# Ones beside the values written once, values split in pieces of 512 columns, and a plan whose clock begins later

## The chip, the core and the metric

The kernel runs on one core of a Trainium2 chip. The core has five engines with a program each: TensorE (PE, matrix products), VectorE (DVE), ScalarE (ACT), GpSimd (POOL) and SyncE (SP, which issues the DMAs). Each engine works through its program in order; one engine waits for another through semaphores. The metric is device microseconds (us) of one execution. Of the kernel before there are three timed runs, with a median of 378.32 us, and one profiled execution.

## The reference

The computation is a chain of three blocks in fp32, for batch 2, 768 positions and 512 channels:

```
scores = q k^T / 8 - slope_h * dist              # 8 heads of 64, keys: 8 global, 96 local
a = softmax(scores where kept, else -1e9);  x = a v      # (2, 768, 512)
h = relu(x w_in);  c = conv over 3 positions of h, per channel
x = (h * sigmoid(c)) w_out                               # (2, 768, 512)
u, v = split(relu(x w_in2));  v = layernorm(v)
x = (u * (w_spatial v + b)) w_out2
```

Each position attends at most to the 8 first keys and to the 96 last ones, so the scores are computed in bands of 256 keys for every 128 queries.

## The kernel before

**The split in halves.** An fp32 matrix is written as a high half in fp16 and a low half, the rest, in fp16 too. A product of two such matrices is three fp16 products: high by high, high by low, low by high. `parts` makes the two halves: a copy to the high half (`copy`, on ACT or DVE), then source minus high half (`minus`, on POOL or DVE; with a scale on DVE alone). Weights arrive from HBM in fp64 and are decoded first (`decode`: POOL, ACT, DVE, DVE), in 16 blocks of w_in and w_out, each 512 KB.

**The attention.** It goes by 6 groups g (2 batches of 3 chunks of 256 positions). A group has 4 pairs of heads, so there are 24 units u, each of two steps of 128 queries: scores on PE (L838), lowest score and difference on DVE (L857), exponential on ACT (L875), turned probabilities, weighing with the values on PE (`weigh`), norm on DVE (L955 to L960), and a turn into the x of the next block (L991). Groups 0 and 1 (`PLAINS`) take values and probabilities in fp32 (L943; the probabilities are turned by PE, L888). Groups 2 to 5 take halves (L949 to L951; the probabilities are turned by a DMA on SP, L914).

**The values.** There is one buffer `v` for the values of a group, in fp32, and two buffers each for `vh` and `vl`, their halves. Each pair of heads has 130 columns in `v` (groups 0, 1) or `vh`: a one, 128 values, a one. The ones make a product with the probabilities give their sum beside the weighed values. `v_load` loads a group; `ones_beside` writes the ones with a memset on POOL; `v_split` makes the halves of groups 2 to 5 (L507 on ACT for `vh`, L519 on DVE for `vl`), and `watch_values` sums squares of `vh` on PE (L796). A load into `v` has to wait until the group before has been read: by `weigh` for groups 0 and 1, by L519 for the others.

**The order.** Nothing runs at once when it is written. Each step is a task of the `Plan`, with a cost for each engine that could do it. `order` makes a list schedule by these costs, several times with other priorities, some of them drawn at random with a fixed seed, and keeps the one that ends first by its own count. The engines' programs are then written in that order, and the engines keep to it, whatever the true times. So a cost that is altered can move instructions everywhere. Behind the plan stands another layer, which puts in the semaphores that the memory accesses need, in the order in which they are written. Where the plan has room on PE in its first 70 us (`WARM_TO`), `emit` fills it with products of no use (`warm`, L1036), into a PSUM bank of their own.

**After the attention** come the first block's products (`inner`, L1065, and `outer`, L1135, which begin during the attention), and the second block (L1219, L1429, L1341, L1491).

Of the kernel before, what the change touches and what calls it, by code (L numbers as in the profile page):

```python
# [23 lines left out]
B, H, S, D = 2, 8, 768, 64  # L24
DM, DFF = 512, 1024
P = 128
NPAIR = H // 2
# [20 lines left out]
NATS, PLAINS = (0, 1, 2), (0, 1)  # L48
# [5 lines left out]
HALF = dict(w=8, x=9, h=12, y=12, g=12, v=8, s=16)  # L54
# [26 lines left out]
def act_bank(n):  # L81
    return 0.06 + 0.00082 * n
# [10 lines left out]
def dve(n):  # L93
    return 0.07 + 0.00105 * n


def beside(n):

    return 0.1 + 0.0022 * n
# [4 lines left out]


def pool(n):
    return 0.15 + 0.0019 * n


def copy_cost(n):  # L110
    return dict(ACT=act(n), DVE=fast(n))


def sub_cost(n):
    return dict(POOL=pool(n), DVE=beside(n))


class Plan:
# [5 lines left out]
    ENGINES = ("PE", "DVE", "ACT", "POOL", "SP")  # L124
    AFTER = dict(PE=0.21, DVE=0.13, ACT=0.14, POOL=0.1, SP=0.03)
    ISSUE, FLIGHT, LANDING, RATE = 0.45, 0.7, 0.9, 0.41e6

    def __init__(self, tc, room):
        self.tc, self.room = tc, room
        self.tasks, self.touched, self.count, self.over, self.slot = [], {}, {}, {}, {}  # L130

    def next(self, kind):
        n = self.count.get(kind, 0)
        self.count[kind] = n + 1
        return kind, n
# [115 lines left out]
    def trial(self, late, total):  # L251

        tasks, after = self.tasks, self.after
        n = len(tasks)
        waits = [len(t[2]) for t in tasks]
        ready = [0.0] * n
        free = dict.fromkeys(self.ENGINES, 0.0)
        banks = [(0.0, k) for k in range(7)] + [(WARM_TO, 7)]
        uses, slots, ended = dict(self.uses), {}, {}
        self.final = final = [0.0] * n  # L260
        dma = 0.0
        open_ = {i for i in range(n) if not waits[i]}
        result = []

        while open_:
            best = None
            for e in self.ENGINES:
                mine = []
                for i in open_:
                    costs = tasks[i][0]  # L270
                    if e not in costs:
                        continue
                    start = max(free[e], ready[i])
                    k = len(self.opens[i])
                    if k:
                        if len(banks) < k:
                            continue
                        start = max(start, banks[k - 1][0])
                    if e == "SP":
                        start = max(start, dma - self.ISSUE - self.FLIGHT - SLACK)  # L280
                        if total:
                            start = max(start, total + late[i] - AHEAD)
                    margin = -MARGIN if e == "DVE" else MARGIN
                    if any(
                        max(free[f], ready[i]) + c + margin < start + costs[e] for f, c in costs.items() if f != e
                    ):
                        continue
                    mine.append((start, i))
                if mine:
                    soon = min(s for s, _ in mine)  # L290
                    rank = lambda i: (
                        late[i] + BIAS * (e == "DVE" and len(tasks[i][0]) > 1)
                        - CLOSE * (e != "PE" and len(self.users[i]) > 0)
                    )
                    i = min((i for s, i in mine if s <= soon + 1e-9), key=rank)
                    soon = next(s for s, j in mine if i == j)
                    if best is None or soon < best[0]:
                        best = soon, e, i
            start, e, i = best
            costs, _, _, load = tasks[i]  # L300
            end = free[e] = start + costs[e]
            if e == "SP":
                dma = max(dma, end + self.FLIGHT) + load
                end = dma + self.LANDING
            result.append((i, e, start))
            final[i] = end
            for k in self.opens[i]:
                slots[k] = banks.pop(0)[1]
            for k in self.users[i]:
                ended[k] = max(ended.get(k, 0.0), end)  # L310
                uses[k] -= 1
                if not uses[k]:
                    banks.append((ended[k] + self.AFTER[e], slots[k]))
                    banks.sort()
            open_.remove(i)
            for j in after[i]:
                waits[j] -= 1
                ready[j] = max(ready[j], end + (0.0 if e == "PE" and "PE" in tasks[j][0] else self.AFTER[e]))
                if not waits[j]:
                    open_.add(j)  # L320
        return result, max(free.values()), slots

    def emit(self, keep=True, warm=None):

        if not keep:
            for costs, emit, _, _ in self.tasks:
                emit(next(iter(costs)))
            return
        block = self.tc.nc.cur_bb.bb
        last = {}  # L330
        seen = len(block.instructions)
        order = self.order()
        when = {i: (start, start + self.tasks[i][0][e]) for i, e, start in order}
        busy, each = 0.0, 0.213
        for i, e, start in order:
            if e == "PE":
                if start < WARM_TO:
                    for _ in range(int((start - busy) / each)):
                        warm()
                    if each > 0.2 and busy > 0:  # L340
                        for _ in range(WARM_AGAIN):
                            warm()
                        each = 0.107
                busy = max(busy, when[i][1])
            self.tasks[i][1](e)
            traced = block.instructions
            for ins in traced[seen:]:
                if ins.engine in last:
                    self.tc.add_manual_dep(
                        ins, last[ins.engine],  # L350
                        mybir.DependencyInfo(mybir.DependencyClass.NoSync, mybir.DependencyReason.DATA),
                        reason="planned order",
                    )
                last[ins.engine] = ins.name
            seen = len(traced)
# [33 lines left out]
class Kernel:  # L389
# [181 lines left out]
    def parts(self, n, hi, lo, src, reads, wh, wl, scale=1.0):  # L571

        add = self.plan.add
        psum = callable(src)
        get = src if psum else lambda: src
        add(
            dict(ACT=act_bank(n), DVE=dve(n)) if psum else copy_cost(n), lambda e: self.copy(e, hi, get(), scale),
            reads=reads, writes=wh,
        )
        add(  # L580
            dict(DVE=dve(n) if psum or n > 512 else dve(n) + 0.3) if psum or scale != 1.0 else sub_cost(n),
            lambda e: self.minus(e, lo, get(), hi, scale),
            reads=list(reads) + list(wh), writes=wl,
        )
# [166 lines left out]
    def v_load(self, g):  # L751
        b, c = divmod(g, NCH)
        n = 3 if c == 0 else 4
        if g in PLAINS:
            v = self.m("v").rearrange("p (n d) -> p n d", d=VW)
            self.ones_beside(v, ("v", g, "one"))
            self.load(
                v[:, : n * NPAIR, 1 : 1 + 2 * D], self.vb[b, c, :, :n].rearrange("p a (n d) -> p (a n) d", d=2 * D),
                [("v", g, "v")], n * P * 2048,
            )  # L760
            return
        v = self.m("v")[:, :2048].rearrange("p (a n) -> p a n", a=4)[:, :n]
        self.load(v, self.vb[b, c, :, :n], [("v", g)], n * P * 2048)
# [11 lines left out]
    def v_split(self, g):  # L775

        if g in PLAINS:
            return
        n = 3 if g % NCH == 0 else 4
        vh, vl = self.v_halves(g)  # L780
        v = self.m("v")[:, : n * 512].rearrange("p (n d) -> p n d", d=2 * D)
        self.ones_beside(vh, ("vh", g, "one"))
        vh, vl = vh[:, : n * NPAIR, 1 : 1 + 2 * D], vl[:, : n * NPAIR]
        self.parts(n * 512, vh, vl, v, [("v", g)], [("vh", g, "v")], [("vl", g, "v")], 2.0 ** HALF["x"])
        self.watch_values(g, vh, n * NPAIR)

    def watch_values(self, g, vh, n):
# [246 lines left out]
    def warm(self):  # L1034

        self.nc.tensor.matmul(self.bank[:, 7, : 2 * P], self.some[:, :P], self.some, start=True, stop=True)  # L1036
# [730 lines left out]
```

## Time and profile before

| what | value |
|---|---|
| timed runs, median (lowest to highest) | 378.32 us (377.89 to 378.91) |
| the profiled execution: time, and span from first to last instruction | 377.42 us, 375.3 us |
| PE busy, share of the span | 356.9 us, 95% |
| ACT, DVE, POOL busy | 275.1, 266.1, 222.4 us (73%, 71%, 59%) |
| mean granted TensorE clock | 0.989 |
| HBM read and written | 31.48 MB, 3.15 MB |

The span is what the trace shows; 2.1 us of the profiled execution's time lie around it. The profiled execution is 0.90 us (0.24%) shorter than the median of the runs. "Busy" for PE is a modelled time: products overlap, and one that is listed with 273 ns follows the one before it by some 110. An engine's idle time is listed with the instruction that it waited for. [...]

### The profile page before, as it was taken

What the parts mean: (1) busy time and instruction counts of PE and PEld (TensorE: products, weight loads), DVE (VectorE), ACT (ScalarE), POOL (GpSimd) and SP (SyncE); (2) the same over time, 40 slices, a digit from 0 to 9 for tenths busy, and PEclk for the clock granted to TensorE, in tenths of its full rate; (3) what the DMA queues carried; (4) which work ended last, traced back from release to release, by engine and by line L of the source; (5) the groups of instructions that cost most, each with busy time, mean ns of one, the idle gap of its engine ahead of it and who ended that gap; (6) DMA issues with size and microseconds to landing.
All of it is one profiled execution on the core that took longest, in us unless ns stands there. A gap on an engine that the chain in (4) does not pass through costs nothing.

```text
span 375.3 us, 8187 instructions
## 1 busy us (share of the span) xinstructions
PE 356.9 (95%) x2928; PEld 255.8 (68%) x2928; DVE 266.1 (71%) x698; ACT 275.1 (73%) x692; POOL 222.4 (59%) x326
## 2 busy tenths in 40 slices
PE   8999499999979999999999999999999999999993
PEld 5787387777768787888788866676546666664442
DVE  5787599558897797999899576357499998881000
ACT  5898499988986898999899566469985846574221
POOL 5654756575468679998866122139985699652000
PEclk9999699999999999999999999999999999999999
DMA  7989511289929796487557000000054000001222
GB/s 222 402 284 290 194 38 38 75 208 224 213 77 220 148 252 186 86 171 213 113 73 211 2 1 2 0 3 0 10 173 152 19 0 2 0 2 56 114 99 79
DMA packets 46257, 43.63 MB, mean 116 GB/s; under 512 B 34816, under 2 KB 36608, under 8 KB 45696
## 3 DMA queue, kind: packets, MB, share of 16 engines
q1 hardware_dynamic: 46208, 43.03, 42.2%
q8 instruction: 25, 0.41, 0.5%
q14 instruction: 24, 0.20, 0.2%
HBM read 31.48 MB, written 3.15 MB: 92 GB/s over the span
## 4 chain that ended last, share of the span: by engine, by line
PE 78%; ACT 7%; DMA 5%; POOL 4%; issue 2%; DVE 2%; SPq 0%; POOLq 0%; ACTq 0%; DVEq 0%
PE bank L1065 13%; PE bank L1341 11%; PE bank L1135 10%; PE bank L1491 8%; PE bank L1429 8%; PE bank L1219 8%; PE bank L838 6%; PE bank L943 5%; DMA v_dt_float<-in_vb 2%; PE bank L1036 2%; DMA pt_dt_float<-ph_dt_float 2%; PE bank L888 2%; POOL hl_dt_float L523 1%; PE bank L949 1%; PE bank L991 1%
## 5 line engine op out<-in xcount | busy, mean ns | idle before, releaser
L1065 PE MATMUL bank<-x_dt_float,w1h_dt_float 128*128 128x260 f16 (+1 forms) x384 | 66.7, 277 | 5.4 <-DVE wk_dt_float L707 5.4
L1135 PE MATMUL bank<-hl_dt_float,w2h_dt_float 128*128 128x254 f16 (+2 forms) x192 | 52.3, 272 | 3.5 <-POOL hl_dt_float L523 3.1
L1065 PE MATMUL bank<-x_dt_float,w1l_dt_float 128*128 128x260 f16 (+1 forms) x192 | 53.0, 276 | 0.0
L1078 DVE SCALAR_TENSOR_TENSOR bank<-hp_dt_float,cwt,bank 128x254 f32<-128x254 f32 (+2 forms) x96 | 46.6, 487 | 8.4 <-ACT bank L1072 5.7
L1135 PE MATMUL bank<-hh_dt_float,w2h_dt_float 128*128 128x254 f16 (+2 forms) x192 | 52.4, 273 | 0.0
L1135 PE MATMUL bank<-hh_dt_float,w2l_dt_float 128*128 128x254 f16 (+2 forms) x192 | 52.3, 272 | 0.0
L523 POOL TENSOR_TENSOR hl_dt_float<-ac_dt_float,hh_dt_float 128x256 f16<-128x256 f32 (+2 forms) x47 | 34.3, 735 | 27.9 <-ACT hh_dt_float L509 24.2
L1065 PEld LDWEIGHTS <-w1h_dt_float 128*128 128x128 f16 x384 | 37.0, 99 | 12.5 <-issue 6.5
L523 POOL TENSOR_TENSOR ph_dt_float<-sb_dt_float,ph_dt_float 128x512 f16<-128x512 f32 x30 | 34.9, 1167 | 13.8 <-ACT ph_dt_float L509 13.4
L857 DVE CUSTOM_DVE_ANT_0 sb_dt_float<-bank,bias_dt_float 128x256 f32<-128x256 f32 (+1 forms) x96 | 35.0, 402 | 10.2 <-PE bank L838 5.8
L1135 PEld LDWEIGHTS <-w2h_dt_float 128*128 128x128 f16 x384 | 36.1, 98 | 7.4 <-issue 1.7
L875 ACT ACTIVATE sb_dt_float<-sb_dt_float,nb_dt_float 128x256 f32<-128x256 f32 (+1 forms) x64 | 29.2, 491 | 9.3 <-POOL nb_dt_float L870 7.0
L1429 PE MATMUL bank<-ys_dt_float,w3uh_dt_float 128*128 128x384 f16 x128 | 31.2, 326 | 0.0
L1491 PE MATMUL bank<-w4h_dt_float,g_dt_float 128*128 128x512 f16 (+1 forms) x104 | 28.9, 363 | 0.0
L1219 PE MATMUL bank<-w3vh_dt_float,ys_dt_float 128*128 128x512 f16 x96 | 28.6, 379 | 0.0
L696 POOL TENSOR_SCALAR raw_dt_float<-raw_dt_float 128x512 int32<-128x512 uint8 x28 | 20.8, 743 | 10.9 <-DMA raw_dt_float<-in_w 9.2
L1491 PEld LDWEIGHTS <-g_dt_float 128*128 128x128 f16 x156 | 15.2, 98 | 15.8
L1341 PE MATMUL bank<-ws_dt_float,vn_dt_float 128*128 128x384 f16 x144 | 24.9, 326 | 0.0
L1219 PEld LDWEIGHTS <-ys_dt_float 128*128 128x128 f16 x144 | 14.1, 98 | 15.6
L1098 ACT ACTIVATE bank<-bank 128x254 f32<-128x254 f32 (+2 forms) x48 | 17.8, 371 | 8.7 <-DVE bank L1078 8.7
L1072 ACT ACTIVATE bank<-hp_dt_float,cwt 128x254 f32<-128x254 f32 (+2 forms) x48 | 23.3, 485 | 0.4
L507 ACT ACTIVATE wk_dt_float<-bank 128x512 f32<-128x512 f32 (+1 forms) x13 | 7.3, 564 | 22.2 <-PE bank L1491 22.2
(182 smaller groups left out, 998.4 us busy)
## 6 DMA issues: line engine op xcount, KB each, us to landing
raw_dt_float<-in_w SPq DMA_DIRECT2D x20, 512.0 KB, 5.4
qk_dt_float<-in_qk SPq DMA_DIRECT2D x24, 336.0 KB, 3.9
v_dt_float<-in_vb SPq DMA_DIRECT2D x4, 1024.0 KB, 5.7
out_x<-wk_dt_float SPq DMA_DIRECT2D x11, 256.0 KB, 2.0
raw_dt_float<-in_wst SPq DMA_DIRECT2D x6, 384.0 KB, 3.9
raw_dt_float<-in_w3v SPq DMA_DIRECT2D x4, 512.0 KB, 5.1
raw_dt_float<-in_w3u SPq DMA_DIRECT2D x4, 512.0 KB, 5.5
v_dt_float<-in_vb SPq DMA_DIRECT2D x2, 768.0 KB, 5.7
```

The lines of the kernel that those rows point to most:

```text
L523: self.engines[e].tensor_tensor(out=out, in0=in0, in1=in1, op=ALU.subtract)
L838: nc.tensor.matmul(self.ps(sp[h])[:, :256], x[r, t * P : (t + 1) * P], y[r, k0 : k0 + 256], start=n == 0, stop=n == len(pairs) - 1,)
L857: nc.vector.tensor_tensor_reduce(out=sb[:, h, :n], in0=self.ps(self.sp[s][h])[:, :n], in1=self.m("bias", 2 * p + h)[:, t0 : t0 + n], scale ...
L875: nc.scalar.activation(out=sb[:, h, :n], in_=sb[:, h, :n], func=AF.Exp, scale=-1.0, bias=nb[:, h : h + 1])
L1065: nc.tensor.matmul(self.ps(acc)[:, :nx], w[f][:, k * P : (k + 1) * P], x[:, k, x0:], start=k == n == 0, stop=k == 3 and n == 2,)
L1072: nc.scalar.activation(out=ac(), in_=near(1), func=AF.Copy, scale=tap(1))
L1078: nc.vector.scalar_tensor_tensor(out=ac(), in0=near(j), scalar=tap(j), in1=ac(), op0=ALU.mult, op1=ALU.add)
L1135: nc.tensor.matmul(ps(), w[2 * d + k // 4][:, k % 4 * P : (k % 4 + 1) * P], x, start=k == n == 0, stop=k == 7 and n == 2,)
L1219: nc.tensor.matmul(ps(), x[:, y, k, tk], w[k], start=n == 0, stop=n == 11)
L1341: self.nc.tensor.matmul(self.ps(acc)[:, :HS], v[:, k, x, ek], w[:, k, y], start=n == 0, stop=n == 8)
L1429: nc.tensor.matmul(ps(), w[e4][:, k * P : (k + 1) * P], x[:, y, k, s], start=n == 0, stop=n == 11)
L1491: nc.tensor.matmul(ps(), x[:, y, k, tk], w[k][:, at], start=n == 0, stop=n == 11)
```

## The change

There are four edits.

1. `v_load` writes the ones beside the values for group 0 alone; groups 1 and those after leave them where they are, and the load names the memset of its group as something to wait for. `v_split` writes them for groups 2 and 3 alone, which are the first users of the two `vh` buffers.
2. `v_split` makes the halves in pieces of 512 columns (one block of 128 keys) in place of 2048 or 1536 at once: 4, 3, 4 and 4 pieces for groups 2 to 5.
3. Costs in the plan: the clock of every engine begins at 0.75 us and that of the DMA at 3.2 us instead of 0; POOL's cost has a further term above 512 columns; a scaled `minus` from SBUF costs 0.1 us over its line instead of 0.3 us (up to 512 columns) or nothing (above).
4. `emit` fills 0.8 of the room on PE with products of no use instead of all of it.

```diff
 def pool(n):
-    return 0.15 + 0.0019 * n
+    return 0.15 + 0.0019 * n + 0.001 * max(n - 512, 0)
...
+    BEGIN, FIRST = 0.75, 3.2
...
-        free = dict.fromkeys(self.ENGINES, 0.0)
+        free = dict.fromkeys(self.ENGINES, self.BEGIN)
...
-        dma = 0.0
+        dma = self.FIRST
...
-                    for _ in range(int((start - busy) / each)):
+                    for _ in range(int(0.8 * (start - busy) / each)):
                         warm()
...
-            dict(DVE=dve(n) if psum or n > 512 else dve(n) + 0.3) if psum or scale != 1.0 else sub_cost(n),
+            dict(DVE=dve(n) if psum else dve(n) + 0.1) if psum or scale != 1.0 else sub_cost(n),
...
             v = self.m("v").rearrange("p (n d) -> p n d", d=VW)
-            self.ones_beside(v, ("v", g, "one"))
+            if g == 0:
+                self.ones_beside(v, ("v", g, "one"))
             self.load(
                 v[:, : n * NPAIR, 1 : 1 + 2 * D], self.vb[b, c, :, :n].rearrange("p a (n d) -> p (a n) d", d=2 * D),
-                [("v", g, "v")], n * P * 2048,
+                [("v", g, "v")], n * P * 2048, [("v", g, "one")],
             )
...
         vh, vl = self.v_halves(g)
-        v = self.m("v")[:, : n * 512].rearrange("p (n d) -> p n d", d=2 * D)
-        self.ones_beside(vh, ("vh", g, "one"))
-        vh, vl = vh[:, : n * NPAIR, 1 : 1 + 2 * D], vl[:, : n * NPAIR]
-        self.parts(n * 512, vh, vl, v, [("v", g)], [("vh", g, "v")], [("vl", g, "v")], 2.0 ** HALF["x"])
+        v = self.m("v")[:, :2048].rearrange("p (n d) -> p n d", d=2 * D)
+        if g - len(PLAINS) < self.m.at["vh"][2]:
+            self.ones_beside(vh, ("vh", g, "one"))
+        vh = vh[:, :, 1 : 1 + 2 * D]
+        for j in range(n):
+            at = slice(j * NPAIR, (j + 1) * NPAIR)
+            self.parts(
+                512, vh[:, at], vl[:, at], v[:, at], [("v", g), ("vh", g, "one")], [("vh", g, "v", j)], [("vl", g, "v", j)],
+                2.0 ** HALF["x"],
+            )
```

**What moves on POOL, while the weights are decoded.** `raw` holds a block of weights as it came, `w1l` is the low half of a block of w_in. In the program before, the second memset of `v`, that of group 1, stands between two blocks:

```order
L696 TENSOR_SCALAR raw_3_dt_float32_134<-raw_3_dt_float32_134 128x512
L696 TENSOR_SCALAR raw_4_dt_float32_139<-raw_4_dt_float32_139 128x512
L768 MEMSET v_0_dt_float32_86 128x16x2
L696 TENSOR_SCALAR raw_5_dt_float32_140<-raw_5_dt_float32_140 128x512
L523 TENSOR_TENSOR w1l_5_dt_float32_100<-wk_1_dt_float32_126,w1h_5_dt_float32_92 128x512
L523 TENSOR_TENSOR w1l_6_dt_float32_101<-wk_2_dt_float32_133,w1h_6_dt_float32_93 128x512
```

In the changed program the same place, with lines numbered one higher there:

```order
L524 TENSOR_TENSOR w1l_4_dt_float32_99<-wk_0_dt_float32_124,w1h_4_dt_float32_91 128x512
L697 TENSOR_SCALAR raw_4_dt_float32_139<-raw_4_dt_float32_139 128x512
L524 TENSOR_TENSOR w1l_5_dt_float32_100<-wk_1_dt_float32_126,w1h_5_dt_float32_92 128x512
L697 TENSOR_SCALAR raw_5_dt_float32_140<-raw_5_dt_float32_140 128x512
L524 TENSOR_TENSOR w1l_6_dt_float32_101<-wk_2_dt_float32_133,w1h_6_dt_float32_93 128x512
```

The memset is gone, and the decoding is followed by the same subtractions, a little interleaved. On PE the program before holds 106 products of no use, the changed one 85.

**What moves on SP, at the first DMA transposes (group 2).** `pt` and `ph` are turned and unturned probabilities, the v load is that of group 2. Before:

```order
L567 DMA qk_0_dt_float32_85<-in_qk 128x672
L914 DMA_TRANSPOSE pt_0_dt_float32_128<-ph_0_dt_float32_201 128x16x128
L567 DMA v_0_dt_float32_86<-in_vb 128x2048
L914 DMA_TRANSPOSE pt_1_dt_float32_141<-ph_1_dt_float32_203 128x16x128
L567 DMA qk_1_dt_float32_119<-in_qk 128x672
L567 DMA qk_2_dt_float32_127<-in_qk 128x672
L567 DMA v_0_dt_float32_86<-in_vb 128x1536
```

Changed:

```order
L568 DMA qk_0_dt_float32_85<-in_qk 128x672
L568 DMA v_0_dt_float32_86<-in_vb 128x2048
L922 DMA_TRANSPOSE pt_0_dt_float32_128<-ph_0_dt_float32_201 128x16x128
L568 DMA qk_1_dt_float32_119<-in_qk 128x672
L922 DMA_TRANSPOSE pt_1_dt_float32_141<-ph_1_dt_float32_203 128x16x128
L568 DMA qk_2_dt_float32_127<-in_qk 128x672
L568 DMA v_0_dt_float32_86<-in_vb 128x1536
```

The load of group 2's values, which waits for the last weighing of group 1, moved ahead of the first transpose, and a load of q and k moved between the two transposes.

**What moves on DVE, where the low half of group 4's values is made** (`x` is the next block's input, `sb` and `nm` belong to scores). Before:

```order
L1103 SCALAR_TENSOR_TENSOR ac_0_dt_float32_176<-bank_74,hp_0_dt_float32_175 128x256
L523 TENSOR_TENSOR x_1_dt_float32_153<-bank_74,x_0_dt_float32_152 128x256 x2
L519 SCALAR_TENSOR_TENSOR vl_0_dt_float32_147<-v_0_dt_float32_86,vh_0_dt_float32_146 128x2048
L857 ISA sb_0_dt_float32_120,nm_3_dt_float32_142<-bank_74,bias_2_dt_float32_79 128x256
L857 ISA nm_3_dt_float32_142 128x1
```

Changed:

```order
L520 SCALAR_TENSOR_TENSOR vl_0_dt_float32_147<-v_0_dt_float32_86,vh_0_dt_float32_146 128x512
L865 ISA sb_0_dt_float32_120,nm_3_dt_float32_142<-bank_74,bias_2_dt_float32_79 128x256
L865 ISA nm_3_dt_float32_142 128x1
L865 ISA sb_0_dt_float32_120,nm_3_dt_float32_142<-bank_74,bias_3_dt_float32_80 128x256
L865 ISA nm_3_dt_float32_142 128x1
L865 ISA sb_1_dt_float32_129,nm_4_dt_float32_144<-bank_74,bias_4_dt_float32_81 128x160
L865 ISA nm_4_dt_float32_144 128x1
L865 ISA sb_1_dt_float32_129,nm_4_dt_float32_144<-bank_74,bias_5_dt_float32_82 128x160
L865 ISA nm_4_dt_float32_144 128x1
L520 SCALAR_TENSOR_TENSOR vl_0_dt_float32_147<-v_0_dt_float32_86,vh_0_dt_float32_146 128x512 x2
L520 SCALAR_TENSOR_TENSOR ys0_0_dt_float32_202<-bank_74,ys0_0_dt_float32_202 128x254
L520 SCALAR_TENSOR_TENSOR vl_0_dt_float32_147<-v_0_dt_float32_86,vh_0_dt_float32_146 128x512
```

One instruction became four, with work for the scores between them. From the first product of the second block (L1219) on, PE's program is the same in both.

## Rows read from the trace of the kernel before

**Rows 1.** The page, part 1: busy us, share of the span, instructions.

```profile
PE 356.9 (95%) x2928; PEld 255.8 (68%) x2928; DVE 266.1 (71%) x698; ACT 275.1 (73%) x692; POOL 222.4 (59%) x326
```

**Rows 2.** Stretches: us, busy of PE, PEld, DVE, ACT, POOL, granted clock, DMA.

```profile
36.70:42.30 5.60, 0.22 (x3) 0.05 (x2) 0.76 (x2) 2.44 (x6) 2.73 (x4) 0.73 0.75 279
42.30:88.00 45.70, 45.70 (x363) 35.88 (x363) 33.95 (x111) 39.31 (x100) 28.80 (x46) 0.96 0.42 98
88.00:160.00 72.00, 67.35 (x793) 55.98 (x792) 62.07 (x180) 61.89 (x152) 53.60 (x75) 1.00 0.74 176
160.00:208.50 48.50, 47.69 (x535) 40.67 (x533) 44.62 (x130) 46.80 (x126) 37.23 (x57) 1.00 0.65 149
208.50:376.00 167.50, 160.79 (x982) 95.70 (x981) 97.42 (x179) 95.70 (x247) 79.01 (x100) 0.99 0.12 40
```

**Rows 3.** Waits of PE: waiter, releaser, total us, times, longest.

```profile
PE bank L1065 <- DVE wk_dt_float L707: 5.4, 1, 5.4
PE bank L1135 <- POOL hl_dt_float L523: 3.1, 3, 2.0
```

**Rows 4.** Timeline 30 to 43 us: start, us, instruction, [idle before it, releaser].

```profile
30.28 0.68 SPq L567 DMA_DIRECT2D v_dt_float<-in_vb  x1
...
39.41 0.14 POOL L768 MEMSET v_dt_float<- 128x32 f32 x1 [6.48 <-DMA v_dt_float<-in_vb]
...
40.35 2.27 POOL L523 TENSOR_TENSOR w1l_dt_float<-wk_dt_float,w1h_dt_float 128x512 f16<-128x512 f32 x2
41.54 0.69 DVE L707 SCALAR_TENSOR_TENSOR wk_dt_float<-raw_dt_float,bank 128x512 int32<-128x512 int32 x1 [6.28 <-POOL w1l_dt_float L523]
...
42.28 0.59 PE L1065 MATMUL bank<-x_dt_float,w1h_dt_float 128*128 128x256 f16 x2 [5.38 <-DVE wk_dt_float L707]
```

**Rows 5.** The chain that ended last: start, us, what.

```profile
30.28 8.68 DMA v_dt_float<-in_vb
...
51.93 1.73 PE bank L943 x16
...
54.30 1.09 PE bank L1036 x9
```

**Rows 6.** Stretches around the idle time of PE, columns as in rows 2.

```profile
33.00:39.30 6.30, 3.90 (x33) 3.06 (x34) 2.26 (x6) 5.68 (x14) 0.00 (x0) 1.00 0.96 305
39.30:46.10 6.80, 3.82 (x19) 2.89 (x19) 4.41 (x11) 1.43 (x4) 6.32 (x10) 0.50 0.49 172
```

**Rows 7.** Timeline where low halves of values are made (107 to 114, 143 to 148).

```profile
108.06 1.63 POOL L523 TENSOR_TENSOR qk_dt_float32r<-qk_dt_float,qh_dt_float32r 128x672 fp32r<-128x672 f32 x1 [0.42 <-ACT qh_dt_float32r L509]
...
108.43 3.41 DVE L519 SCALAR_TENSOR_TENSOR vl_dt_float<-v_dt_float,vh_dt_float 128x2048 f16<-128x2048 f32 x1
...
109.64 2.73 POOL L523 TENSOR_TENSOR hl_dt_float<-ac_dt_float,hh_dt_float 128x256 f16<-128x256 f32 x1
...
113.44 0.67 POOL L523 TENSOR_TENSOR hl_dt_float<-ac_dt_float,hh_dt_float 128x256 f16<-128x256 f32 x1
...
143.72 2.28 DVE L519 SCALAR_TENSOR_TENSOR vl_dt_float<-v_dt_float,vh_dt_float 128x2048 f16<-128x2048 f32 x1
...
143.94 2.58 POOL L696 TENSOR_SCALAR raw_dt_float<-raw_dt_float 128x512 int32<-128x512 uint8 x1
```

**Rows 8.** Groups by line and shape: count, busy us, mean ns, idle before.

```profile
L519 DVE SCALAR_TENSOR_TENSOR ws_dt_float<-raw_dt_float,ws_dt_float 128x384 f16<-128x384 f32 x9 | 7.6, 866 | 0.0
...
L507 ACT ACTIVATE vh_dt_float<-v_dt_float 128x2048 f16<-128x2048 f32 x3 | 5.7, 1913 | 1.6 <-DMA v_dt_float<-in_vb 1.6
...
L509 ACT CAST w1h_dt_float<-wk_dt_float 128x512 f16<-128x512 f32 x8 | 4.6, 617 | 0.0
```

**Rows 9.** Timeline of SP, 70 to 100 us, columns as in rows 4.

```profile
75.96 3.15 SPq L914 DMA_TRANSPOSE pt_dt_float<-ph_dt_float  x1
79.22 0.52 SPq L567 DMA_DIRECT2D v_dt_float<-in_vb  x1
79.84 5.19 SPq L914 DMA_TRANSPOSE pt_dt_float<-ph_dt_float  x1
```

## The prediction

> **What bounds the kernel now.** I read the page's first part, then busy time by stretches, then who made PE wait, then the timeline and the chain around the longest wait. PE is busy for 356.9 of 375.3 us and no other engine passes 73% [rows 1], so time is gained where PE stands still, runs at the low clock, or does work of no use. By stretches [rows 2], PE is full from 42.3 to 88 us, loses 4.7 of 72 us from 88 to 160, 0.8 of 48.5 after that, and is full again until the tail; from 36.7 to 42.3 it works 0.2 of 5.6 us. So the trace has one big hole and some small ones. The list of PE's waits puts 5.4 us on one wait, that of a product of the first block for DVE at L707, and 3.1 us on three waits for a low half on POOL [rows 3].
>
> The big hole is a convoy, followed back in [rows 4]: PE waits 5.38 us for L707 on DVE; that instruction waited 6.28 us for a `w1l` on POOL; and POOL stood in front of the memset of `v` for 6.48 us, until the load of group 1's values had landed. [Rows 5]: that load took 8.68 us from its issue at 30.28. The memset writes columns that the load doesn't touch, yet it waited for it. Nothing that POOL had behind it needed the values.
>
> [...]
>
> **The change part by part.** The sum is made against the profiled execution, 377.4 us, which is 0.9 us under the median of the runs.
>
> *The memset of group 1 goes.* POOL then goes on at 32.9 us (39.41 less 6.48) with decoding and with `w1l`, and L707 no longer comes at 41.54. Upper bound of the gain: the whole 5.4 us. What is late next: ACT has 39.3 us of work in the 45.7 after the hole and did 2.4 of 5.6 in it [rows 2], so from 36.7 to 88 it has 41.7 us of work; pressed into 51.3 less 8.4 (this, the clock and half of the warm products below), 42.9 us, it would be 97% busy, as it already is from 160 to 208.5 (46.8 of 48.5). It will hold PE up now and then; I leave 1.0 us of the hole: **-4.4** (bounds -5.4 and, if ACT gives back most of it, -2). The group's load is needed by the weighing at 51.93 [rows 5]; it landed at 38.96. With the hole and the slow clock gone that weighing comes some 8.5 us earlier, near 43.4, so the load stays hidden by 4 us. The first load now waits for its memset in name, but the memset moved ahead of the identity on POOL; behind that load on SP stand only loads, and I cost it at nothing.
>
> *The slow clock.* 3.8 us of work at half speed would take 1.9 at full speed: **-1.9** (bounds -1.9 and 0; if PE again stands still long enough, it comes back).
>
> *Fewer products of no use.* 106 become 85. Nine of them take 1.09 us of the chain [rows 5], 0.12 each, so 21 are 2.5 us at most. Some only covered time in which PE would have waited. No row tells which; I take half, **-1.2** (bounds -2.5; and +3.4 if the thinner filling lets the clock fall for one more stretch as long as that of [rows 6], 6.8 us at half speed).
>
> *Values in pieces, ACT and DVE.* On ACT, three instructions of 2048 columns took 1.91 us each [rows 8], so with the one of 1536 some 7.2 in all; 15 casts of 512 columns at 0.617 are 9.3: +2.1 us on an engine with 10 us free from 88 to 160. On DVE no row has the piece. Bounds: 2.28 us for 2048 columns with no wait in it [rows 7] gives 0.57 a piece, 15 pieces 8.6; the 384 columns of `ws` at 0.866 in a stretch where POOL is busy [rows 8] give 1.15 a piece, 17.3 in all. Before, three and three quarters times 2.28 and the 1.13 that one of them waited (below) make 9.7. So -1.1 to +7.6 us on DVE, which has 9.9 us free from 88 to 160. I take 0.8 a piece, nearer to the quiet row since ACT's pace spaces the pieces: +2.3, hidden but for **+0.5**.
>
> *Values in pieces, POOL.* This is where I expect a second gain. [Rows 7]: the low half at 108.43 took 3.41 us, 1.13 more than its like at 143.72; POOL was in a subtraction until 109.69. And POOL's next one, 0.67 us when undisturbed (113.44), took 2.73, until the long DVE instruction had ended. At 143.94 it happens again: 2.58 us for a step of decoding, ended with DVE's. So the two shut each other out, for a whole instruction, and two of PE's three waits for POOL [rows 3] fall right behind. In pieces, POOL is held for about 0.6 us at a time and can slip between. Of 3.1 us I take **-2.0** (bounds -3.1 and 0). [...]
>
> [...]
>
> *The new plan.* PE's products are the same ones in a slightly other order. One place worries me: SP. Before, the first transpose was issued at 75.96, the load of group 2's values at 79.22, the second transpose at 79.84 [rows 9]. Now the load stands ahead of both, and a transpose holds SP for 3.2 to 5.2 us, so the second one goes out later than before in relation to the load. Two weighings that stand together on PE need both. Bounds 0 and +5.2 (one such issue); I take **+1.5**, since the load itself gains some 2 us. The other edits of costs change only which order was found; no row prices them, and they lie in the range.
>
> Sum: -4.4 - 1.9 - 1.2 + 0.5 - 2.0 + 1.5 = -7.5. Of 377.4 that leaves 369.9; with the 0.9 us to the median, **370.8 us**.
>
> **The rivals.**
> A. *All of it comes through.* ACT gives nothing back and SP costs nothing: -5.4 - 1.9 - 2.5 - 3.1 = -12.9, 364.5, or 365.4 by the median. For it: PE has no wait at all from 42.3 to 88. Against: ACT would have to be 97% busy.
> B. *ACT becomes the bound before 88 us.* The hole is replaced by many small waits: only 2 of 5.4 us, the clock, and half of what POOL gives; SP as above: -2 - 1.9 - 1.0 + 0.5 + 1.5 = -2.9, 374.5, or 375.4. For it: ACT's load. Against: DVE takes copies too, and had 4.8 us idle in the hole.
> C. *The transfer was the bound anyway:* PE meets the load of group 1 at the weighing instead of through POOL, and nothing is gained: 378.3. It would need the load to land near 50 instead of 38.96; the DMA share of 0.96 from 33 to 39.3 [rows 6] speaks for late loads, the 4 us in hand against.
> D. *Slower: the pieces queue behind POOL.* From 88 to 160 each of 15 pieces may wait for a whole POOL instruction, up to 1.63 us [rows 7], and DVE, in order, holds up scores and the first block's steps behind it. DVE has 9.9 us free there; what is gained before (hole, clock, half the warm products) is at most 8.4. So it decides from (9.9 + 8.4) / 15 = 1.22 us a piece. Halfway to 1.63, at 1.43, it costs 21.4 - 9.9 - 8.4 = +3.1: 380.5, or 381.4 by the median. Against: POOL is busy 74% there, and not every instruction is a long one.
> That the change doesn't do what it says is hardly open for the memset: it is not in the built order.
>
> **How the numbers follow.** Forecast 0.52, A 0.16, B 0.18, C 0.06, D 0.08. The forecast's own range is 367 to 374. The range is to hold 8 in 10: from 365, A's end, to 377, past B, with D and most of C left out. A measurement of this kernel can tell some 0.3% from no change, here 1.1 us. Faster than that: forecast, A and most of B, 0.85. Within it: C and a little of B, 0.07. Slower: D, 0.08.
>
> **What would show it.** In the changed kernel's trace POOL has no wait for the load of `v`; PE has no idle stretch over 2 us before 88 us, and the granted clock stays at 1.00 between 36 and 50. No subtraction on POOL of 256 columns takes over 1.5 us from 88 to 160, and PE waits under 1.5 us in all for POOL there. Pieces on DVE of 0.6 to 0.9 us on the mean bear the term out; over 1.2 is D. A wait of PE for a transpose of 1 to 2 us at the first weighing of group 2 is my SP term. The forecast is wrong if the full stretch that begins at 208.5 us [rows 2] comes forward by less than 4 us.

## The result and the profile after

| | kernel before | changed kernel |
|---|---|---|
| median of 4 runs, us | 378.51 | 373.6 |
| lowest and highest, us | 377.89, 378.91 | 371.49, 378.51 |
| profiled execution, us (span) | 377.42 (375.3) | 373.29 (371.4) |
| mean granted clock there | 0.989 | 0.992 |

The ratio of the times is 0.9853, 95% interval 0.9808 to 0.9898: faster by 1.5%, or 5.6 us. (The run of 378.51 was disturbed and is not in the ratio.) The forecast was 370.8 us, with a range of 365 to 377.

The first part of the page of the changed kernel, as [rows 1]: PE works 2.2 us less, DVE 3.2 us more.

```profile
PE 354.7 (95%) x2907; PEld 253.5 (68%) x2907; DVE 269.3 (73%) x709; ACT 277.0 (75%) x707; POOL 220.5 (59%) x319
```

Waits of PE in the changed kernel, as [rows 3]: waiter, releaser, total us, times, longest.

```profile
PE bank L957 <- DMA pt_dt_float<-ph_dt_float: 4.2, 3, 2.4
PE bank L999 <- DVE wk_dt_float L708: 1.7, 1, 1.7
PE bank L951 <- DVE ac_dt_float L1111: 1.3, 1, 1.3
...
PE bank L896 <- ACT pt_dt_float L510: 1.1, 1, 1.1
PE bank L804 <- ACT vh_dt_float L508: 0.5, 1, 0.5
...
PE bank L1143 <- POOL hl_dt_float L524: 0.2, 1, 0.2
```

The 5.4 us for DVE and nearly all of the 3.1 us for POOL are gone. New at the top are 4.2 us for transposes of P.

The timeline where the hole was, as [rows 4]:

```profile
29.64 0.68 SPq L568 DMA_DIRECT2D v_dt_float<-in_vb  x1
...
32.11 1.16 POOL L524 TENSOR_TENSOR w1l_dt_float<-wk_dt_float,w1h_dt_float 128x512 f16<-128x512 f32 x1
...
33.55 0.68 POOL L697 TENSOR_SCALAR raw_dt_float<-raw_dt_float 128x512 int32<-128x512 uint8 x1 [0.29 <-DMA raw_dt_float<-in_w]
...
34.31 2.29 POOL L524 TENSOR_TENSOR w1l_dt_float<-wk_dt_float,w1h_dt_float 128x512 f16<-128x512 f32 x2
...
37.74 0.66 PE L896 MATMUL bank<-ident,sb_dt_float 128*128 128x128 f32 x4 [1.10 <-ACT pt_dt_float L510]
...
44.70 0.99 PE L951 MATMUL bank<-v_dt_float,pt_dt_float 128*128 128x65 f32 x7 [1.29 <-DVE ac_dt_float L1111]
```

The load of values goes out as before, but POOL goes on behind it. The sixth `w1l` begins at 32.11 and the last two at 34.31; in the kernel before, the sixth and seventh began together at 40.35 [rows 4]. PE waits twice in places where it did not before, 1.10 and 1.29 us. The weighing that stood at 51.93 [rows 5] begins at 44.70.

Busy time by stretches of the changed kernel, columns as in [rows 2]; the last two rows are from inside the third:

```profile
36.37:45.00 8.63, 6.24 (x52) 4.63 (x49) 7.00 (x18) 7.76 (x21) 4.56 (x11) 1.00 0.63 238
45.00:82.00 37.00, 36.95 (x305) 28.20 (x304) 29.86 (x94) 34.50 (x92) 21.31 (x32) 1.00 0.45 104
82.00:160.00 78.00, 71.32 (x806) 58.85 (x804) 65.36 (x196) 66.05 (x167) 58.17 (x81) 0.98 0.71 171
204.60:371.00 166.40, 160.84 (x984) 95.69 (x981) 99.20 (x182) 96.35 (x248) 77.48 (x97) 0.99 0.12 40
...
115.00:118.50 3.50, 1.19 (x12) 0.73 (x10) 1.30 (x6) 1.18 (x5) 0.70 (x1) 1.00 1.22 189
...
120.00:123.50 3.50, 3.50 (x19) 2.46 (x18) 0.76 (x4) 2.32 (x6) 2.84 (x4) 0.51 0.88 211
```

The low clock of [rows 6] has left its place: the first two rows have 1.00. But a new hole at 115 to 118.5 is followed by 3.5 us at 0.51. By the weighing at 44.70 the kernel is 7.2 us ahead; where the full stretch begins (204.6 against 208.5) 3.9 are left. So 3.3 us are lost between: from 82 to 160 PE stands still for 6.7 us, where in the kernel before it stood still for 4.7 from 88 to 160 [rows 2], and the low clock takes 1.7.

### The profile page after: what moved, and what is told of

Its sections match the earlier page's. It is cut to its first block, busy times and chain, and to the rows that moved or that the text cites. A ratio compares the mean times of both kernels' runs of the same rounds, so it can differ in the third digit from the quotient of the medians.

```text
span 371.4 us, 8158 instructions
## 1 busy us (share of the span) xinstructions
PE 354.7 (95%) x2907; PEld 253.5 (68%) x2907; DVE 269.3 (73%) x709; ACT 277.0 (75%) x707; POOL 220.5 (59%) x319
## 4 chain that ended last, share of the span: by engine, by line
PE 78%; DMA 8%; ACT 5%; DVE 3%; POOL 2%; issue 1%; SPq 0%; ACTq 0%; POOLq 0%
PE bank L1073 13%; PE bank L1143 11%; PE bank L1349 11%; PE bank L1499 8%; PE bank L1437 8%; PE bank L1227 8%; PE bank L846 5%; PE bank L951 5%; DMA pt_dt_float<-ph_dt_float 4%; DMA v_dt_float<-in_vb 3%; PE bank L896 2%; PE bank L1044 2%; PE bank L999 1%; PE bank L957 1%; ACT sb_dt_float L883 1%
## 5 line engine op out<-in xcount | busy, mean ns | idle before, releaser
L524 POOL TENSOR_TENSOR hl_dt_float<-ac_dt_float,hh_dt_float 128x254 f16<-128x254 f32 (+2 forms) x48 | 33.5, 706 | 22.0 <-ACT hh_dt_float L510 20.9
L524 POOL TENSOR_TENSOR ph_dt_float<-sb_dt_float,ph_dt_float 128x512 f16<-128x512 f32 x32 | 37.8, 1183 | 13.7 <-ACT ph_dt_float L510 11.9
L697 POOL TENSOR_SCALAR raw_dt_float<-raw_dt_float 128x512 int32<-128x512 uint8 x28 | 19.0, 680 | 15.1 <-DMA raw_dt_float<-in_w 6.3
L1416 ACT ACTIVATE hp_dt_float<-bank 128x260 f32<-128x260 f32 (+1 forms) x48 | 18.9, 393 | 5.0 <-PE bank L1073 5.0
```

What stands on the lines that cost most here:

```text
L524: self.engines[e].tensor_tensor(out=out, in0=in0, in1=in1, op=ALU.subtract)
L697: nc.gpsimd.tensor_scalar(out=lo, in0=top, scalar1=1.0 / 32, scalar2=1.0 / 64 - 0.5, op0=ALU.mult, op1=ALU.add)
```

## The experiments

Each ratio is to the kernel before, run on the same chip. "Same order" means that the plan is as in the kernel named, and only what an instruction does, or whether it is there, is changed.

| run | what it is | median, us | ratio | 95% interval |
|---|---|---|---|---|
| b_silent | before, same order, no second memset | 373.65 | 0.9839 | 0.9795 to 0.9884 |
| b_warm08 | before, same order, 25 warm products fewer | 380.73 | 1.0014 | 0.9985 to 1.0044 |
| b_pieces | before, same order, splits in runs of 512 | 380.76 | 1.0030 | 1.0005 to 1.0055 |
| a_v5 | changed, one load behind a transpose | 371.95 | 0.9800 | 0.9762 to 0.9838 |
| a_again | changed, once more | 373.39 | 0.9849 | 0.9796 to 0.9901 |
| a_warm1 | changed, same order, 22 warm products more | 372.44 | 0.9839 | 0.9786 to 0.9892 |
| a_noclock | changed, plan's clock at zero, new plan | 372.97 | 0.9833 | 0.9781 to 0.9886 |
| a_whole | changed, whole splits, new plan | 368.08 | 0.9709 | 0.9662 to 0.9756 |
| a_s4, a_s6 | changed, plan's slack 0.4 and 0.6 | 369.79, 371.92 | 0.9713, 0.9786 | ±0.0049, ±0.0046 |
| w_s4, w_s6 | whole splits, slack 0.4 and 0.6 | 367.75, 374.06 | 0.9669, 0.9830 | ±0.0047, ±0.0049 |

The first four runs of the table were made together, and so were the next four and the last four.

**b_silent: the memset alone.**

```
-        self.plan.add(dict(POOL=0.08), lambda e: self.nc.gpsimd.memset(out, 1.0), writes=[name])
+        emit = lambda e: None if name == ("v", 1, "one") else self.nc.gpsimd.memset(out, 1.0)
+        self.plan.add(dict(POOL=0.08), emit, writes=[name])
```

> The kernel before, its order of instructions unchanged, without the second memset of the ones columns beside the first plain values (the columns hold ones from the first memset). Theory (the memset's wait for the value load held POOL, then DVE, then TensorE, and the clock fell for it): the 5.4 us idle of TensorE ahead of L1065 goes down to under 1 us, no stretch at 0.50 granted clock between 36 and 50 us, and the time falls by 5 to 7 us to 371 to 373. Rival B (ACT's work before 88 us is late next and takes half of it back): falls by 2.5 to 4 us to 374 to 376, with new waits of TensorE for ACT between 45 and 88 us. Rival C (the value load itself was the bound): within 1 us of 378.

One memset of 0.14 us less [rows 4] is 1.6% of the kernel. The longest waits of PE in this run:

```profile
PE bank L1136 <- POOL hl_dt_float L523: 3.1, 3, 2.0
PE bank L1037 <- DVE hl_dt_float L591: 1.2, 1, 1.2
PE bank L992 <- DVE r_dt_float L956: 0.9, 1, 0.9
PE bank L797 <- ACT vh_dt_float L507: 0.7, 1, 0.7
```

And two stretches of it, columns as in [rows 2]: the place of the old hole, and the end of the longest wait that is left.

```profile
36.00:50.00 14.00, 14.00 (x119) 11.62 (x118) 13.14 (x37) 13.76 (x37) 9.82 (x20) 1.00 0.50 183
103.00:106.00 3.00, 0.97 (x10) 0.71 (x9) 3.00 (x6) 1.29 (x3) 3.00 (x3) 1.00 0.38 115
...
107.00:110.60 3.60, 3.60 (x25) 2.66 (x23) 2.56 (x8) 2.85 (x8) 3.57 (x7) 0.56 0.97 301
```

From 36 to 50 us PE works all of 14.00 us at full clock, with ACT busy for 13.76 of them: ACT is as full as I had feared, and yet PE waits for no one. The 5.4 us wait is gone whole and nothing takes its place before 85 us. That speaks against rival B, and rival C is out. The waits for POOL hl are untouched, and the longest is now followed by a low clock.

**b_warm08 and a_warm1: the warm products.**

```
-                    for _ in range(int((start - busy) / each)):
+                    for _ in range(int(0.8 * (start - busy) / each)):
```

> The kernel before, its order unchanged, with 0.8 times the warm products that its plan puts into TensorE's free time (some 22 fewer). Theory (half of them stand where TensorE is late against its plan, so each is 0.109 us on the path): 0.6 to 1.6 us faster, 376.7 to 377.7. Rival (all of them are on the path): 2.3 us faster, 376.0. Rival (they only fill waits): within 0.4 us. Rival (fewer products let the clock fall in one more stretch): 1 to 4 us slower, with a stretch of 0.50 granted clock that before does not have.

> The changed kernel, its order unchanged, with all the warm products of its plan (factor 1.0 in place of 0.8, 22 more). Theory as predicted (half of them on the path): 1.0 to 1.5 us slower than the changed kernel run beside it. Rival (as the kernel before with the factor alone showed: they only fill TensorE's waits): within 0.5 us of it. Rival (all on the path): 2.3 us slower.

The first takes this edit alone into the kernel before, the second takes it out of the changed kernel. 25 products fewer give 1.0014, 22 more give 0.9839 against 0.9849 of the changed kernel beside it. Neither is told from no change, and the second differs in the wrong direction. In the kernel before, the 1.2 us that I expected lie outside the interval (0.6 us faster to 1.7 slower); for the changed kernel 0.5% either way stays open. One rival is left: the runs with fewer products have the lower mean granted clock in both pairs (0.985 against 0.987 over the runs of b_warm08 and of the kernel before, 0.990 against 0.993 for a_again and a_warm1). By my estimate from these means that is some 1 us each, about what the term should have given. In its profiled execution b_warm08 has a stretch at the low clock from 113 to 117 us that the one of the kernel before hasn't, as the slow rival had it; but b_silent, with all its products, has one behind the same wait for POOL. So the runs show that thinning them gave no time, not whether the products only covered waits.

**b_pieces: the pieces alone.**

```
-        self.parts(n * 512, vh, vl, v, [("v", g)], [("vh", g, "v")], [("vl", g, "v")], 2.0 ** HALF["x"])
+        pieces = [slice(j * NPAIR, (j + 1) * NPAIR) for j in range(n)]
+        def copies(e):
+            for at in pieces:
+                self.copy(e, vh[:, at], v[:, at], 2.0 ** HALF["x"])
...
+        self.plan.add(dict(DVE=dve(n * 512)), rests, reads=[("v", g), ("vh", g, "v")], writes=[("vl", g, "v")])
```

> The kernel before, its order unchanged, where each split of values issues its ACT copies and its DVE subtractions in runs of 512 columns in place of one instruction of 2048 or 1536. Theory (a long subtraction on DVE shuts POOL out while it runs, and POOL's late hl pieces hold TensorE; short ones let POOL in between): the three waits of TensorE for POOL hl, 3.1 us in sum, fall under 1 us, pieces take 0.7 to 0.9 us, and the time falls by 1 to 3 us to 375.3 to 377.3. Rival D (each piece waits its turn behind POOL, over 1.2 us a piece): 1 to 3 us slower. Rival (the run of four shuts POOL out just as the one did): within 0.5 us, the waits stay at 2.5 us or more.

The waits for POOL hl did fall, from 3.1 to 0.4 us, and the kernel got 0.3% slower. The timeline of b_pieces at the place of [rows 7] shows both:

```profile
109.84 5.52 DVE L519 SCALAR_TENSOR_TENSOR vl_dt_float<-v_dt_float,vh_dt_float 128x512 f16<-128x512 f32 x4
111.05 1.13 POOL L523 TENSOR_TENSOR hl_dt_float<-ac_dt_float,hh_dt_float 128x256 f16<-128x256 f32 x1
112.14 1.60 POOL L523 TENSOR_TENSOR ph_dt_float<-sb_dt_float,ph_dt_float 128x512 f16<-128x512 f32 x1
...
115.29 0.41 DVE L868 CUSTOM_DVE_ANT_0 sb_dt_float<-bank,bias_dt_float 128x256 f32<-128x256 f32 x1
...
115.76 0.27 PE L1146 MATMUL bank<-hh_dt_float,w2h_dt_float 128*128 128x256 f16 x1 [2.82 <-DVE nm_dt_float L868]
```

POOL's `hl` takes 1.13 us where it took 2.73. The four pieces take 5.52 us where the one took 3.41: POOL slips between them, and DVE pays for it. What DVE has behind them, the scores' minima at L868, comes later, and PE waits 2.82 us for those in place of 2.0 for `hl`. In waits this is a draw. The runs' mean granted clock is 0.983 against 0.987, which by my estimate is 1.4 us, enough for the 1.1 us that the kernel lost; that the pieces lowered it isn't shown.

**a_v5: one load behind a transpose.**

```
         order = self.order()
+        for load, turn in ((873, 689),):
+            order.insert([x[0] for x in order].index(turn), order.pop([x[0] for x in order].index(load)))
```

> The kernel after the change, with one load of 2048 columns of values (the fifth) issued behind the thirteenth transpose of P in place of three DMAs ahead of it; nothing else moves. Theory (this load and the transpose share the DMA engines, so that the transpose lands 7.3 us after its issue against 4.3 alone; TensorE waits 2.4 us for it at 116 to 118 us and the clock falls for it): transpose 4 to 5 us, that wait under 0.5 us, no 0.50 clock at 120 to 123 us, and 2 to 4 us faster than the changed kernel's 373.3, 369.5 to 371.3. Rival (the wait only moves to the next transpose or to the later load's split): 372.5 to 374, with waits for pt or vh of 2 us or more after 118 us.

The timeline of the changed kernel, and behind it that of a_v5:

```profile
109.89 0.33 SPq L568 DMA_DIRECT2D v_dt_float<-in_vb  x1
111.18 4.11 SPq L922 DMA_TRANSPOSE pt_dt_float<-ph_dt_float  x1
...
118.56 0.20 PE L957 MATMUL bank<-vh_dt_float,pt_dt_float 128*128 128x65 f16 x1 [2.38 <-DMA pt_dt_float<-ph_dt_float]
```

```profile
110.96 1.89 SPq L924 DMA_TRANSPOSE pt_dt_float<-ph_dt_float  x1
112.95 1.46 SPq L570 DMA_DIRECT2D v_dt_float<-in_vb  x1
...
116.35 0.20 PE L959 MATMUL bank<-vh_dt_float,pt_dt_float 128*128 128x65 f16 x1 [0.39 <-DMA pt_dt_float<-ph_dt_float]
```

With the 1 MB load ahead of it the transpose landed 7.3 us after its issue, without it 5.3. PE waits 0.39 in place of 2.38 us, and this execution has no stretch at the low clock there. So the load's part in the late transpose is shown, though 4 to 5 us were expected for the landing. Part of the wait moved: behind 118 us PE now waits three times for DVE's minima (L867), 1.9 us in all and 1.10 at the longest, less than the 2 us that the rival had named. The ratio, 0.9800 against 0.9849 and 0.9853, is lower by 1.9 us, just under the 2 to 4 expected, and the intervals overlap: likely, not settled.

**a_again** and **a_noclock: the changed kernel, and its plan without the clock.**

> The changed kernel itself, as the measure for the three kernels beside it and to see how often its 2.4 us wait for a transpose at 116 us lowers the clock. Theory: ratio to the kernel before 0.983 to 0.988; the wait for a transposed P at the thirteenth weighing is there again (1.5 us or more), with or without a 0.50 clock behind it. Rival (the wait is an accident of one execution): under 0.5 us, and the time like that of the kernel with the fifth value load moved, 371 to 372.5.

```
-    BEGIN, FIRST = 0.75, 3.2
+    BEGIN, FIRST = 0.0, 0.0
```

> The changed kernel with the plan's two starting times (engines, DMA) at zero as before; the order is planned anew. Theory (the second memset carries the gain and the rest of the plan only moves waits about): within 1.5 us of the changed kernel run beside it, no TensorE wait over 2 us and no 0.50 clock between 36 and 50 us. Rival (the true starting time is what lets loads and engines come in time): 2 us or more slower, with TensorE waits for DMA or w1 before 60 us that the changed kernel doesn't have.

The wait for the transpose is there again, 2.6 us, with a stretch at 0.50 behind it. The plan's clock makes another order, in which PE waits elsewhere (2.5 us at 41 us for the first block's sums on DVE, L1111, and 0.50 clock right behind it), and no difference in time that can be told: 0.9833 against 0.9849. That wait and that clock were not expected; only the time was.

**a_whole: whole splits in a new plan.**

```
-        for j in range(n):
-            at = slice(j * NPAIR, (j + 1) * NPAIR)
-            self.parts(
-                512, vh[:, at], vl[:, at], v[:, at], [("v", g), ("vh", g, "one")], [("vh", g, "v", j)], [("vl", g, "v", j)],
...
+        self.parts(
+            n * 512, vh[:, : n * NPAIR], vl[:, : n * NPAIR], v[:, : n * NPAIR], [("v", g), ("vh", g, "one")],
+            [("vh", g, "v")], [("vl", g, "v")], 2.0 ** HALF["x"],
+        )
```

> The changed kernel with each split of values whole again (one ACT copy and one DVE subtraction of 2048 or 1536 columns); the order is planned anew. Theory (pieces pay where the plan puts short DVE and POOL work between them, since a long subtraction shuts POOL out): TensorE's waits for POOL hl or for DVE work behind the long subtraction come back, 2 to 3 us, and the time is 1 to 3 us above the changed kernel's. Rival (pieces only move the cost from POOL to DVE, as a run of them did in the order before): within 0.7 us of the changed kernel. Rival (pieces cost DVE more than they give): 1 us or more faster.

My theory failed: it is 1.4% faster than the changed kernel, and faster than both kernels of the case. The waits of PE in a_whole, in full those over 0.5 us:

```profile
PE bank L1143 <- POOL hl_dt_float L524: 1.6, 3, 0.8
PE bank L1044 <- DVE hl_dt_float L592: 1.2, 1, 1.2
PE bank L896 <- ACT pt_dt_float L510: 0.9, 1, 0.9
PE bank L957 <- DMA pt_dt_float<-ph_dt_float: 0.7, 2, 0.5
```

POOL's waits are in part back, 1.6 us, but those for transposes are 0.7 in place of 4.2 and those for DVE's L708 gone. And with whole splits the order alone has halved the 3.1 us for POOL. The gain can come from the pieces' absence, or from the order that was found; the last four runs ask which.

**a_s4, a_s6, w_s4, w_s6: the same work in other orders.** One constant that bears on SP's issues alone.

```
-ROUNDS, SLACK, AHEAD, MARGIN, BIAS, CLOSE = 6, 0.5, 60.0, 1.0, 10.0, 15.0
+ROUNDS, SLACK, AHEAD, MARGIN, BIAS, CLOSE = 6, 0.4, 60.0, 1.0, 10.0, 15.0
```

> The changed kernel (values in pieces of 512) with one constant of the plan moved that has nothing to do with the values (the slack of the DMA queue's issues, 0.4 in place of 0.5): another order of the same work, to see what planning anew alone does to the time. Theory (the pieces themselves cost, on DVE and POOL): within 1.5 us of the changed kernel, ratio to the kernel before 0.981 to 0.989. Rival (the changed kernel's order was an unlucky draw, its waits for transposes above all): 2 us or more faster than it, ratio under 0.979, near the kernel with whole splits.

> As the run beside it, with the slack at 0.6. Theory (pieces cost): ratio to the kernel before 0.981 to 0.989. Rival (unlucky draw): under 0.979.

> The changed kernel with whole splits of values and the slack at 0.4. Theory (whole splits are cheaper in any order): ratio to the kernel before 0.967 to 0.976, 3 to 5 us under the kernel in pieces with the same slack. Rival (the 368.1 us of whole splits was a lucky draw): ratio 0.978 or more, level with the kernel in pieces of the same slack.

> As the run with whole splits beside it, with the slack at 0.6. Theory: ratio 0.967 to 0.976, 3 to 5 us under the kernel in pieces with the same slack. Rival (lucky draw): 0.978 or more.

In pieces the three orders give 0.9713, 0.9786 and 0.9849, whole 0.9669, 0.9709 and 0.9830. The spread inside each (0.014 and 0.016) is as large as what I had asked after, and at slack 0.6 whole splits are the slower of the two by their medians. So 368.1 us was partly a lucky draw and 373.4 an unlucky one. Whether pieces cost anything in a planned order stays open: the means differ by 0.005. What goes with the good draws are the waits for transposes: 0.7 us in all in a_whole and in a_s4, 4.2 in the changed kernel, 3.1 in w_s6. They don't explain all of it, as w_s4 has 1.0 and a_s6 1.1. For whole splits the low clock explains more: in the profiled executions of a_whole, w_s4 and w_s6, with spans of 365.2, 367.1 and 372.9 us, an estimate of what it cost (each stretch's length times the share of the clock that is missing) is 0, 1.7 and 6.9 us, nearly the whole spread. In pieces it is not so: a_s6, a_s4 and the changed kernel lost 0, 3.4 and 1.7 us so, with spans of 367.5, 368.6 and 371.4.

## Why the prediction was right, and where it was not

The direction, the main cause and the range were right; the time came out 2.8 us above the forecast (by the ratio a gain of 5.6 us, where 7.5 were forecast). By its own terms, with the two profiled executions (377.4 to 373.3) and the runs:

- *Hole, -4.4.* Right in kind. With the order kept the whole 5.4 us wait goes (b_silent), so the 1.0 us left for ACT wasn't needed there; in the changed kernel's order two new waits of 1.10 and 1.29 us take 2.4 back, so the term is -3.0 in the profiles. One wait is for ACT, the other for DVE. The load landed 10.3 us after its issue at 29.64, still 4.8 us ahead of the weighing at 44.70, so it stayed hidden as said.
- *Slow clock, -1.9.* The 3.8 us of work run from 42.28, where PE works again [rows 4], to the end of the 0.50 at 46.1 [rows 6]. That the work goes at half speed there shows in the chain of the kernel before, where twelve products of L1065 take 2.72 us in that stretch and 1.31 us at 1.00:

```profile
42.28 2.72 PE bank L1065 x12
...
55.90 1.31 PE bank L1065 x12
```

  In the changed kernel the low clock is gone from its place, but back, as its bound allowed ("if PE again stands still long enough, it comes back"): 3.5 us at 0.51 from 120 are 1.7 us. In the profiles this term is -0.2.
- *Warm products, -1.2.* Failed. PE worked less by it, and the end didn't move (b_warm08, a_warm1). The step that failed is the half that I took without a row ("No row tells which; I take half"). In its place the runs show no gain in the order before, 0.6 us faster to 1.7 slower, and in the changed kernel's order nothing that can be told from none. Whether the products only covered time, or a lower clock took back what they cost, stays open.
- *Pieces on POOL, -2.0.* In the changed kernel the waits for POOL are 0.2 us, and POOL's `hl` falls with the pieces (b_pieces), so it was read rightly that the long DVE instruction shut POOL out: `hl` takes 1.13 us there where it took 2.73 [rows 7]. But b_pieces shows that in the order before the gain was no gain: what POOL no longer waits, DVE does. I wrote that POOL "can slip between" and costed DVE's side at +2.3 us, hidden but for +0.5; in one stretch alone it was 2.1 us (5.52 against 3.41), and it came out as a wait of PE for DVE. This step failed on the side that I had called nearly free.
- *Pieces on DVE, 0.8 us each.* The group in the changed kernel is below: 1.04 us mean, over my band of 0.6 to 0.9.

```profile
L520 DVE SCALAR_TENSOR_TENSOR vl_dt_float<-v_dt_float,vh_dt_float 128x512 f16<-128x512 f32 x15 | 15.2, 1035 | 2.6 <-ACT vh_dt_float L508 2.5
```

  Eight pieces take 0.68 to 0.70 us each, 0.69 on the mean. The other seven take 1.04 to 1.91 us, and each of them begins while POOL is in a subtraction. Rival D's mechanism is there, then, but small: its 1.22 us was worked out as waiting for each piece, and here that is 0.35 on the mean (1.04 less 0.69). The sign "over 1.2 is D" put the whole piece against it, which was a slip. At one place the waiting reaches PE:

```profile
147.47 1.51 DVE L520 SCALAR_TENSOR_TENSOR vl_dt_float<-v_dt_float,vh_dt_float 128x512 f16<-128x512 f32 x1
148.39 2.06 POOL L524 TENSOR_TENSOR qk_dt_float32r<-qk_dt_float,qh_dt_float32r 128x672 fp32r<-128x672 f32 x1
148.91 1.56 DVE L878 TENSOR_TENSOR nb_dt_float<-nm_dt_float,shift 128x2 f32<-128x2 f32 x1
...
151.11 0.69 DVE L708 SCALAR_TENSOR_TENSOR wk_dt_float<-raw_dt_float,bank 128x512 int32<-128x512 int32 x1
151.86 0.33 PE L999 MATMUL bank<-ident,xk_dt_float 128*128 128x128 f32 x1 [1.70 <-DVE wk_dt_float L708]
```

  The piece takes twice its 0.7 us, and behind it even a subtraction of two columns (L878) takes 1.56 us, until POOL's of 148.39 is over. L708 is late, and PE waits 1.70 us.
- *New plan, +1.5.* Mis-sized: 4.2 us of waits for transposes against 0.6 before, +3.6, inside its bound of 5.2. The place that I named cost 1.17 us, as said; the larger one, 2.38 us at 118.56, I hadn't seen. A load of values stands close ahead of a transpose in both places. At the first, PE waits for the next transpose, which SP could issue only at 77.96; at the second for that transpose itself, which landed late, and a_v5 takes that wait away.

Of the signs listed: no wait of POOL for `v`, no idle stretch of PE over 2 us before 88, clock 1.00 from 36 to 50, and POOL's waits are as said. The pieces' mean fits neither of its two bands. The full stretch came forward by 3.9 us, and I had called the forecast wrong under 4: by that sign it failed, narrowly. A slip without consequence: 5.4, 1.9 and 1.2 are 8.5, where the prediction has 8.4 twice.

The profiles' 3.9 us can be added up from PE's rows: hole -3.0, waits for POOL -2.9, for transposes +3.6, for L708 +1.7, smaller waits -1.1, PE's own work -2.2. That says where PE's time went in two traces, not what each edit is worth. What carried the forecast is the hole: as far as the intervals tell, the whole of the measured gain is that one memset, 0.9839 alone, 0.9849 and 0.9853 with all the rest.

How near 373.6 is to 370.8 is partly luck. Three orders of the same changed work gave 0.9713 to 0.9849, which against 378.5 us is 367.6 to 372.8; the prediction had put the choice of order into its range without a price. The better orders beat the memset alone (0.9839) by about 1%. Whether edits 2 to 4 or only the draw give that is open: the kernel before was not planned anew without its memset, and the altered costs of POOL and of `minus` were not run alone.

## What to carry to other kernels

When an engine in the middle of a chain stands in front of an instruction that itself takes 0.14 us, ask what that instruction waits for and what is queued behind it: taking it out was worth 6 us here, more than any other edit that a run tried alone in a kept order. In b_pieces shorter instructions took PE's waits for POOL from 3.1 to 0.4 us but handed the lost time to the other engine, with a wait of 2.82 us for DVE in their place; before cutting instructions up, look at what that engine has behind them. Where a planner makes the order, one order of each version proves little: run each version in a few orders before crediting an edit with 1%.

## What the hardware showed that was not expected

- The low clock is not tied to a long wait in a simple way. The 2.0 us wait for POOL left the clock at 1.00 from 88 to 160 in the kernel before [rows 2] and was followed by 3.6 us at 0.56 in b_silent. In a_s4 the longest wait of PE is 1.2 us, at the very start, and the windows from 8 to 24 us show PE busy throughout; and yet a stretch at half clock follows, columns as in [rows 2]:

```profile
24.00:31.00 7.00, 7.00 (x34) 6.11 (x34) 5.12 (x13) 3.96 (x10) 2.60 (x4) 0.52 0.51 173
```

  In a_whole, a_v5, a_s6 and a_warm1 the profiled executions show 1.00 from 8 to 364 us, though a_warm1 has a wait of 1.8 us. By the same estimate as above half of such a stretch is lost, 1.7 to 3.4 us, and not in every execution: two runs of a_s4 at a mean clock of 0.996 and 0.997 took 367.2 us, the profiled one at 0.986 took 370.4. What decides it wasn't tried.
- The 1 MB load costs the transpose behind it, in both places where the two changed places: in a_v5 the thirteenth took 5.3 us in place of 7.3, and the first DMA transpose, ahead of the load in the kernel before (75.96) and behind it in the changed one (72.23), took 5.4 and 7.1. The load isn't the only cause: the changed kernel has one of 7.2 us at 138.5 with no load of values near.
